# Attention followed by a GELU layer pair: batch 2 reordered in the GELU staging buffer, three transposes moved, left-over keys on VectorE, another start

## The chip, the cores and the metric

The kernel runs on 1 core of one Trainium2 chip. The metric is device microseconds of one execution. Times are medians of several runs. A ratio is the mean time of one kernel's fast runs over the mean of the other's fast runs in the same rounds, so it is not quite the ratio of the medians quoted beside it. "Chain of work" means the chain of instructions that ended last, followed back from the end.

## The reference, cut to what matters

```python
q, k, v: (8 batches, 12 heads, 448 positions, 64)      # float32
scores = q @ k^T / 8
attn = exp(scores - m) / (sum(exp(scores - m)) + exp(-m) + 1e-9)
x = (attn @ v) as 3584 rows of 768
h = x @ w_in                                            # 768 -> 2048
out = (0.5 * h * (1 + erf(h / sqrt 2))) @ w_out         # 2048 -> 768
```

## The kernel before: the parts that the change touches

Two heads make a pair, six pairs a batch, and a step is the attention of one pair, so there are 48 steps. 448 keys are three blocks of 128 and 64 left-over keys. Steps 1 to 6 (batch 0) are the opening. In later steps the two layers of the batch before lie between the parts of a step. Queries and keys of batches 0 and 1 are transposed by TensorE, those of later batches by DMA.

The start: the loads of the first two pairs, with the second pair held back behind small memsets, and narrow warm-up matmuls.

```python
    load_first(0, nc.sync, nc.scalar)          # pair 0: queries on the sync queue, keys on ScalarE's
    load_table(SET_LN_EXP)
    ...
    for t in (first_q[1], first_k[1]):
        nc.vector.memset(t[:, 0, 0, 0:1], 0.0)
    load_first(1, nc.sync, nc.sync)            # pair 1, after those memsets
    load_left(kl_raw, k, 0)                    # from here on GpSimd's queue
    ...
    for _ in range(54):
        nc.tensor.matmul(warm[0:D, 0:D], ones, ones, start=True, stop=True)
    ...
    load_q(1); load_k(1); load_left(kl_raw, k, 1)   # batch 1, ahead of all weights
    for i in range(4):
        load_w_in(i, 4)
```

One step of the opening. Denominators of the left-over keys come from a second pair of matmuls with `ones_left`:

```python
    def start_step(s):
        ps = presum_items(s)                   # six VectorE adds; the last two are the left-over keys
        for j in range(NK):
            scores(s, j)                       # and their exponentials on ScalarE
        if s >= 2:
            normalize(s - 2)
        ...
        if s + 1 < NPAIR:
            transpose_on_pe(0, s + 1)
        for c in {NPAIR - 2: (0,), NPAIR - 1: (1, 2, 3)}.get(s, ()):
            transpose_on_pe(1, c)
        ps[0](); ps[1]()
        scores_left(s)
        if s >= 1:
            values(s - 1)
            denominators(s - 1, left=et_t.pop(s - 1)[:, 2 * NK])
            log_den(s - 1)
            exp_den(s - 1)
        for p in ps[2:4]:
            p()
```

Batch 2 comes in by wide loads and is put in order by VectorE for the transposing DMA. Before, the ordered copy takes the raw buffer of batch 1, so batch 1 must be transposed completely by then:

```python
        if b not in ordered[w]:
            ordered[w][b] = raw_pool.tile([n, H, nj, D], FP16, name=name)
    ...
    step(NPAIR + 1, mlp1(0, 2, 6))
    transpose_on_pe(1, NPAIR - 1)
    gelu_window(0, 6)                          # first layer with its GELU, from a staging buffer "hbuf"
    fetch(0, -1)                               # orders the first half of batch 2
```

Only two PSUM buffers ("bank") serve transposes, values, denominators and both layers; three ("st") serve the scores.

The softmax here doesn't subtract the row's maximum and nothing guards it: scores larger than these inputs give would overflow.

## Time and profile before

| | kernel before |
|---|---|
| time | 416.02 us (415.27 to 416.29, 3 runs) |
| profiled run | 415.54 us, span 413.8 us |
| TensorE busy | 400.6 us (97%) |
| ScalarE busy | 300.5 us (73%) |
| VectorE busy | 196.0 us (47%) |
| GpSimd busy (issuing loads) | 102.2 us (25%) |

The page gives busy tenths for 40 slices of some 10 us; the slices in which TensorE's row is not full show where time can be won. A timeline line is: start, length, engine, source line, operation, output and inputs, shape, count, and in brackets how long the engine was idle just before and on whom it waited. The lines of the kernel before stand in the prediction below. Here is one more for later comparison, from the timeline of its TensorE: the key transposes of batch 1's first pair, with no wait on a load.

```profile
24.95 0.37 PE L243 MATMUL bank<-ident,rawk 128*64 128x128 f16 x6
```

### The profile page before, as it was taken

Reading aid. Unit: us, or ns where it says so; the run is one execution under the profiler, and the core shown is the slowest. Engines: PE = TensorE matmul, PEld = TensorE weight load, DVE = VectorE, ACT = ScalarE, POOL = GpSimd, SP = SyncE. Lnnn points to the kernel's source line nnn. Section 1 sums busy time; section 2 is a strip of 40 time slices with the busy share of each in tenths; the row PEclk is TensorE's granted clock in tenths of the full one; section 3 lists DMA queues with packets and bytes.
Section 4 is the critical chain, followed back from the end, with each engine's and each line's share of the span. In section 5 each row is a group of like instructions: output and inputs, shape, how many; then the busy total and the mean of one; then the engine's idle time right before and its main releaser. Section 6 shows DMA issues by size and latency. Waiting matters only on the chain.

```text
span 413.8 us, 10452 instructions
## 1 busy us (share of the span) xinstructions
PE 400.6 (97%) x4450; PEld 251.9 (61%) x4450; DVE 196.0 (47%) x471; ACT 300.5 (73%) x450; POOL 102.2 (25%) x137
## 2 busy tenths in 40 slices
PE   6789999999999999999999999999999999999996
PEld 4455755556556665556655566556566565687784
DVE  5666346873366604674256722576146741530021
ACT  5998779979897747978687766998588676734300
POOL 9732420674704540055201650020000000000000
PEclk9999999999999999999999999999999999999999
DMA  9999999999954996189921999159011100110022
GB/s 156 190 202 200 198 194 165 174 176 169 160 87 70 163 164 68 43 99 146 140 59 56 146 144 113 43 78 173 21 40 47 32 25 16 53 52 16 2 79 76
DMA packets 136671, 43.78 MB, mean 106 GB/s; under 512 B 117744, under 2 KB 136624, under 8 KB 136624
## 3 DMA queue, kind: packets, MB, share of 16 engines
q0 software_dynamic: 91440, 22.39, 58.1%
q1 hardware_dynamic: 44912, 20.52, 27.6%
q8 instruction: 35, 0.57, 0.6%
q10 hardware_dynamic: 272, 0.20, 0.1%
q14 instruction: 12, 0.10, 0.1%
HBM read 45.61 MB, written 11.01 MB: 137 GB/s over the span
## 4 chain that ended last, share of the span: by engine, by line
PE 90%; ACT 5%; DVE 2%; DMA 1%; issue 0%; SPq 0%; DVEq 0%
PE bank L230 73%; PE st L321 7%; PE bank L369 6%; ACT et L311 3%; PE st L230 2%; PE st L377 2%; DMA hbuf<-in_k_dram 1%; ACT rec L386 1%; ACT rec L389 1%; DVE xt L395 0%; DVE tqk L250 0%; ACT L72 0%; PE bank L238 0%; PE bank L243 0%; DVE vl L168 0%
## 5 line engine op out<-in xcount | busy, mean ns | idle before, releaser
L311 ACT ACTIVATE et<-st,expb 128x896 f16<-128x896 f32 x192 | 160.4, 913 | 34.1 <-PE st L321 25.6
L230 PE MATMUL bank<-xt,w_in_sb 128*64 128x448 f16 x1536 | 152.6, 353 | 0.5 <-DVE hbuf L423 0.3
L230 PEld LDWEIGHTS <-w_in_sb 128*64 128x64 f16 x1536 | 92.6, 110 | 56.2 <-issue 6.7
L230 PE MATMUL bank<-w_out_sb,gt_odd 128*64 128x384 f16 x1024 | 88.2, 327 | 0.0
L460 DVE COPY osb<-bank 128x384 f32<-128x384 f32 x56 | 31.2, 558 | 113.6 <-PE bank L230 113.6
L230 PEld LDWEIGHTS <-gt_odd 128*64 128x64 f16 x1024 | 60.6, 110 | 25.7 <-issue 4.5
L230 PE MATMUL bank<-w_out_sb,gt_even 128*64 128x384 f16 x768 | 68.9, 327 | 0.0
L395 DVE TENSOR_TENSOR xt<-bank,rec 128x448 f16<-128x448 f32 x48 | 29.8, 620 | 64.9 <-PE bank L369 46.6
L230 PEld LDWEIGHTS <-gt_even 128*64 128x64 f16 x768 | 43.5, 110 | 22.9 <-issue 4.4
L419 ACT ACTIVATE gt_odd<-bank 128x448 f16<-128x448 f32 (+1 forms) x74 | 29.1, 394 | 23.0 <-PE bank L230 21.9
L423 DVE COPY hbuf<-bank 128x448 f32<-128x448 f32 x54 | 33.7, 623 | 16.4 <-PE bank L230 15.2
L321 PE MATMUL st<-tqk 64*128 64x448 f16 x288 | 38.0, 362 | 1.8 <-ACT rec L386 0.7
L110 POOL DMA_DIRECT2D rawq<-in_q_dram x40 | 30.7, 786 | 35.5 <-DVE rawq L264 18.6
L369 PE MATMUL bank<-et,vn 128*64 128x448 f16 x288 | 35.5, 352 | 0.0
L355 DVE TENSOR_TENSOR t<-et 128x448 f16<-128x448 f16 x96 | 33.2, 388 | 2.5 <-ACT et L311 1.2
L355 DVE TENSOR_TENSOR ksum<-t,et 128x448 f16<-128x448 f16 x96 | 34.0, 384 | 0.6 <-ACT et L311 0.4
L419 ACT ACTIVATE gt_even<-bank 128x384 f16<-128x384 f32 x34 | 16.7, 490 | 23.0 <-PE bank L230 23.0
L355 DVE TENSOR_TENSOR ksum<-ksum,et 64x448 f16<-64x448 f16 x84 | 32.0, 382 | 1.3
L96 POOL DMA_DIRECT2D vn<-in_v_dram x9 | 8.9, 991 | 92.6 <-PE st L321 89.3
L110 POOL DMA_DIRECT2D rawk<-in_k_dram x30 | 24.6, 824 | 19.3 <-DMA rawq<-in_q_dram 15.3
L386 ACT ACTIVATE rec<-st,oneb 128x448 f32<-128x448 f32 x42 | 27.1, 647 | 2.8 <-PE st L377 2.8
L389 ACT ACTIVATE rec<-rec 128x448 f32<-128x448 f32 x48 | 27.6, 577 | 1.5
(58 smaller groups left out, 237.9 us busy)
## 6 DMA issues: line engine op xcount, KB each, us to landing
vn<-in_v_dram POOLq DMA_DIRECT2D x7, 576.0 KB, 9.1
rawq<-in_q_dram POOLq DMA_DIRECT2D x40, 84.0 KB, 10.7
rawk<-in_k_dram POOLq DMA_DIRECT2D x32, 96.0 KB, 8.0
w_in_sb<-in_moe_w_in_dram POOLq DMA_DIRECT2D x4, 768.0 KB, 18.8
w_out_sb<-in_moe_w_out_dram POOLq DMA_DIRECT2D x4, 768.0 KB, 21.3
out_dram<-osb SPq DMA_DIRECT2D x16, 168.0 KB, 3.7
out_dram<-osb SPq DMA_DIRECT2D x16, 144.0 KB, 2.1
out_dram<-osb SPq DMA_DIRECT2D x16, 120.0 KB, 2.0
```

The lines of the kernel that those rows point to most:

```text
L110: nc.gpsimd.dma_start(out=dst[:, :, j, e, :], in_=view[j, e])
L230: nc.tensor.matmul(out[x], lhs[:, x], rhs, start=start, stop=stop)
L311: nc.scalar.activation(out=out, in_=in_, func=AF.Exp, bias=expb, scale=scale)
L321: nc.tensor.matmul(st[:, e, 0:S], kt[r, j, :], qt[r], start=True, stop=True)
L355: nc.vector.tensor_tensor(out=dst, in0=a, in1=x, op=ALU.add)
L369: nc.tensor.matmul(po_t[g][e * D:(e + 1) * D, 0:S], v_t[b][:, 2 * c + e, j, :], et[:, 2 * j + e], start=False, stop=(j == NK - 1),)
L386: nc.scalar.activation(out=rec_t[g], in_=den_t.pop(g)[:, 0:S], func=AF.Ln, bias=oneb, scale=1.0)
L389: nc.scalar.activation(out=rec_t[g], in_=rec_t[g], func=AF.Exp, scale=-1.0)
L395: nc.vector.tensor_tensor(out=xt_t[b][:, c, :], in0=po_t.pop(g)[:, 0:S], in1=rec_t.pop(g), op=ALU.mult)
L419: nc.scalar.activation(out=dst[:, 0, :], in_=ph[:, c0:c1], func=AF.Gelu)
L423: nc.vector.tensor_copy(out=h_t[b][:, fc, :], in_=ph[:, 0:S])
L460: nc.vector.tensor_copy(out=osb, in_=po[:, 0:NHW])
```

## The change

Its intent: start the second pair's loads at once; keep the array's warm-up wide; take the left-over keys' denominators off TensorE; and put the ordered copy of batch 2 into the GELU staging buffer, so that batch 1's transposes can spread into later steps and the last of them lies beside the first second-layer item. The diff is cut to what matters. "Set n" below is the transposes of batch 1's pair n, counted from 0: `transpose_on_pe(1, n)`.

```diff
@@ load_pairs
         tiles[b] = raw_pool.tile([n, H, nj, D], FP16, name=name)
+        if b == 3:
+            nc.vector.memset(tiles[b][:, 0, 0, 0:1], 0.0)
@@ the start
-    load_first(0, nc.sync, nc.scalar)
-    load_table(SET_LN_EXP)
+    for i, queue in enumerate((nc.sync, nc.scalar)):
+        queue.dma_start(out=first_q[i], ...)
+        nc.scalar.dma_start(out=first_k[i], ...)
+        if i == 0:
+            load_table(SET_LN_EXP)
-    for t in (kl_raw[0], vl[0], kl_raw[1], vl[1]):
+    for t in (kl_raw[1], kl_raw[0], vl[0], vl[1]):          # now ahead of "ones"
         nc.vector.memset(t, 0.0)
-    ones_left = ...                                          # and its three memsets
-    for t in (first_q[1], first_k[1]):
-        nc.vector.memset(t[:, 0, 0, 0:1], 0.0)
-    load_first(1, nc.sync, nc.sync)
-    for _ in range(54):
-        nc.tensor.matmul(warm[0:D, 0:D], ones, ones, start=True, stop=True)
+    for _ in range(7):
+        nc.tensor.matmul(warm, kl_raw[1][:, 0],
+            kl_raw[1].rearrange("p c x -> p (c x)")[:, 0:512], start=True, stop=True)
@@ order_by_pairs
-        if b not in ordered[w]:
-            ordered[w][b] = raw_pool.tile([n, H, nj, D], FP16, name=name)
+        if b not in ordered[0]:
+            spare = h_pool.tile([P, 2 * NBURST * S], FP16, name="hbuf")
+            ...                                              # queries and keys side by side in it
@@ start_step
-        for c in {NPAIR - 2: (0,), NPAIR - 1: (1, 2, 3)}.get(s, ()):
+        for c in {NPAIR - 2: (0,), NPAIR - 1: (1, 2)}.get(s, ()):
-            denominators(s - 1, left=et_t.pop(s - 1)[:, 2 * NK])
+            denominators(s - 1)
-        for p in ps[2:4]:
+        for p in ps[2:]:
@@ the seventh and eighth step
-    transpose_on_pe(1, NPAIR - 2)
-    denominators(s - 1, left=et_t[s - 1][:, 2 * NK])
+    transpose_on_pe(1, NPAIR - 3)
+    denominators(s - 1)
+    transpose_on_pe(1, NPAIR - 2)
     step(NPAIR + 1, mlp1(0, 2, 6))
-    transpose_on_pe(1, NPAIR - 1)
@@ after the step with the first second-layer item
+        if b == 0 and r == 0:
+            transpose_on_pe(1, NPAIR - 1)
```

More of the change, by code (lines that the diff above doesn't have):

```diff
@@ L152 @@
         for n, nj, x, w in ((PS, NJ, 0, 512), (P, NK, 1024, 384)))
-    def load_first(i, queue_q, queue_k):
+    for i, queue in enumerate((nc.sync, nc.scalar)):
         h2 = slice(2 * i, 2 * i + 2)
-        queue_q.dma_start(
+        queue.dma_start(
             out=first_q[i], in_=q[0, h2, 0:PS * NJ].rearrange("h (p j) d -> p h j d", j=NJ))
-        queue_k.dma_start(
+        nc.scalar.dma_start(
             out=first_k[i], in_=k[0, h2, 0:P * NK].rearrange("h (p j) d -> p h j d", j=NK))
-    load_first(0, nc.sync, nc.scalar)
-    load_table(SET_LN_EXP)
+        if i == 0:
+            load_table(SET_LN_EXP)
     ident = const.tile([P, P], FP16, name="ident")
     make_identity(nc, ident)
+    for t in (kl_raw[1], kl_raw[0], vl[0], vl[1]):
+        nc.vector.memset(t, 0.0)
     ones = const.tile([P, D], FP16, name="ones")
     nc.vector.memset(ones, 1.0)
-    for t in (kl_raw[0], vl[0], kl_raw[1], vl[1]):
-        nc.vector.memset(t, 0.0)
-    ones_left = const.tile([P, P], FP16, name="ones_left")
-    nc.vector.memset(ones_left, 0.0)
-    for e in range(2):
-        r = slice(e * LEFT, (e + 1) * LEFT)
-        nc.vector.memset(ones_left[r, e * D:(e + 1) * D], 1.0)
     expb = const.tile([P, 1], FP32, name="expb")
@@ L186 @@
     warm = ps_bank.tile([P, 512], FP32, name="bank")
-    for _ in range(54):
-        nc.tensor.matmul(warm[0:D, 0:D], ones, ones, start=True, stop=True)
+    for _ in range(7):
+        nc.tensor.matmul(
+            warm, kl_raw[1][:, 0], kl_raw[1].rearrange("p c x -> p (c x)")[:, 0:512],
+            start=True, stop=True)
     load_v(0, 0, 4)
@@ L255, in order_by_pairs @@
     def order_by_pairs(b, w, c0, c1):
-        n, nj, raw, name = ((PS, NJ, q_raw, "rawq"), (P, NK, k_raw, "rawk"))[w]
-        if b not in ordered[w]:
-            ordered[w][b] = raw_pool.tile([n, H, nj, D], FP16, name=name)
+        nj, raw = ((NJ, q_raw), (NK, k_raw))[w]
+        if b not in ordered[0]:
+            spare = h_pool.tile([P, 2 * NBURST * S], FP16, name="hbuf")
+            for i, (rows, chunks, x) in enumerate(((PS, NJ, 0), (P, NK, H * NJ * D))):
+                ordered[i][b] = spare[0:rows, x:x + H * chunks * D].rearrange(
+                    "p (h j d) -> p h j d", h=H, j=chunks)
         src = raw[b].rearrange("p (c e) j d -> p c e j d", e=2)
@@ L363, in values @@
         b, c = divmod(g, NPAIR)
-        et = et_t.pop(g) if b else et_t[g]
+        et = et_t.pop(g)
         po_t[g] = ps_bank.tile([P, 512], FP32, name="bank")
@@ L372, in values, with denominators @@
                 )
-    def denominators(g, bank=None, left=None):
+    def denominators(g, bank=None):
         den_t[g] = ps_bank.tile([P, 512], FP32, name="bank") if bank is None else bank
@@ L378, in denominators @@
                 den_t[g][e * D:(e + 1) * D, 0:S], ones, sum_t[g][:, e, :],
-                start=True, stop=left is None)
-        if left is not None:
-            matmul_cols(den_t[g][:, 0:S], ones_left, left, False, True)
+                start=True, stop=True)
         del sum_t[g]
@@ L593 @@
     values(s - 1)
-    del et_t[s - 1]
     normalize(s - 1)
```

## The prediction

> **What bounds the kernel now.** I read the page first (busy tenths and clock), then the chain of work in order of time, then the timelines of the single engines in the stretches that the diff touches, and last the issue and landing times of the DMAs. The page's slices:
>
> ```profile
> span 413.8 us, 10452 instructions
> PE   6789999999999999999999999999999999999996
> ACT  5998779979897747978687766998588676734300
> PEclk9999999999999999999999999999999999999999
> ```
>
> TensorE is full from the fifth slice on (from about 40 us); only the first 40 us have holes. There the second row shows ScalarE near full. The chain for that part, pieces of it:
>
> ```profile
> 3.53 4.73 DMA hbuf<-in_k_dram
> 8.90 0.54 PE bank L243 x6
> 9.58 0.67 DVE tqk L250
> 10.30 1.30 PE st L321 x6
> ...
> 19.70 1.39 ACT et L311 x2
> ...
> 33.12 0.64 DVE xt L395
> 33.79 0.38 PE bank L377 x2
> 34.17 0.20 PE bank L230 x2
> 34.40 0.64 ACT rec L386
> ...
> 43.84 0.64 DVE hbuf L423
> 44.52 11.55 PE bank L230 x120
> ```
>
> (start, length, what). So there are four limits in turn: to 11 us the loads of the first heads, above all the second key load, which is only issued at 3.53 and lands at 8.27; to about 31 us ScalarE's exponentials; from 31 to 38 us a ping-pong in which ScalarE waits for TensorE; then TensorE to the end. A gain after 45 us needs less TensorE work or a closed hole; a gain before needs an earlier load or less ScalarE idle time. ScalarE at the start, with its idle time in brackets:
>
> ```profile
> 6.61 2.80 ACT L311 ACTIVATE et<-st,expb 128x896 f16<-128x896 f32 x3 [0.65 <-PE st L321]
> 9.96 0.63 ACT L311 ACTIVATE et<-st,expb 128x448 f16<-128x448 f32 x1 [0.54 <-PE st L230]
> 10.89 3.33 ACT L311 ACTIVATE et<-st,expb 128x896 f16<-128x896 f32 x4 [0.31 <-PE st L321]
> ```
>
> After the first exponential there are only 0.54 + 0.31 = 0.85 us of holes up to 31.6 us; the five later opening steps repeat every 4.345 us (19.61, 23.95, 28.30) without a hole. The two places further on where the diff can act:
>
> ```profile
> 33.79 0.38 PE L377 MATMUL bank<-ksum,ones 128*64 128x448 f16 x2 [0.65 <-DVE xt L395]
> 44.52 1.70 PE L230 MATMUL bank<-xt,w_in_sb 128*64 128x448 f16 x16 [0.29 <-DVE hbuf L423]
> 61.92 0.36 PE L321 MATMUL st<-tqk 64*128 64x448 f16 x2 [0.68 <-ACT rec L386]
> ```
>
> The last is a TensorE hole of 0.68 us right after the first second-layer item: the third score tile of the next step waits until the logarithm has given its bank back.
>
> **What the Trainium skill says.** "TensorE: Matmul & The Clock Gate", Part 1: the array starts at half rate and is released after a window of sustained activity of about 3.4 us. This trace agrees in kind, but its clock record shows 0.5 only up to 12.5 us although 54 narrow warm-up matmuls ran from 0.99 to 4.08; eight query transposes take 0.59 us before that and 0.40 after. "DMA: Bandwidth & Descriptors", section Issuing engines are not separate DMA queues: DMAs from all issuers interleave on the same 16 engines, so another issuing queue saves only issue time. Same page, section Queues, rings and completion order: each engine takes turns between queue rows. The trace fits: the first pair (224 and 192 KB, alone) landed in 3.3 and 3.6 us, the second, beside GpSimd's loads, in 4.3 and 4.7. "TensorEngine Tiling (Array Packing)", section Key Properties: tiles work independently. Here a pair of 64-column matmuls of 448 columns advances the chain by 0.19 us though each is recorded with some 0.35.
>
> **The change part by part.**
>
> *The start.* The second query load moves from the sync queue to ScalarE's queue and no longer waits for the small memsets at 3.05, and the second key load follows it. They sit behind the first key load on that queue, so the first pair should land as before (4.08 and 4.30), at worst some tenths later, because the second query load shares the engines with the tail of the first (224 against 192 KB: 32 KB). I take issue times of 1.3 to 2.9 us (the table load, 1.21 to 2.49, stands between in program order) instead of 3.16 and 3.53, and landings near 6 and 6.5 to 7 instead of 7.45 and 8.27. The transposes of pair 1 can then follow the scores of pair 0 directly at about 7.5 instead of 8.25 and 8.90. The left-over exponential of pair 0 would start when the three before it end (9.42, not 9.96) and those of pair 1 at 9.42 + 0.63 = 10.05, not 10.89. That is at most 0.85. The seven wide warm-up matmuls (512 columns at the slow rate, estimated from 448 columns in 0.38 to 0.43 us: about 3 us) start after the first 0.38 us memset, end near 4.3, before the first transposes at 4.78, and use the whole array, so the clock may be released well before 12.5; that would shorten the chain from landing to first exponential (transposes, scores: some 1.2 us of TensorE) by 0.2 to 0.4. Against it: the first left-over key load waits for the second memset now (about 0.4 later), and contention. Net: **-0.8 us**.
>
> *Left-over keys on VectorE.* Six steps lose two matmuls each, 0.19 us of TensorE per step, and gain two VectorE adds of 64x448, 0.38 each, 0.79 together. In steps 1 to 4 TensorE is not the limit, so nothing is gained. The adds fit: in the step at 18 us the partial sums end at 18.76, the left-over exponential at 18.57, the adds would run to 19.55, and the next VectorE work (normalize) starts at 19.73 behind the exponential of the logarithm. Slack 0.18 us, so no loss either. In the last two steps ScalarE does wait for the denominators (0.23 before 31.84 and 0.42 before 34.40), there 0.19 is won.
>
> *Transposes of batch 1.* Each set costs TensorE 0.56 us (29.11 to 29.67) and VectorE a copy of 0.65. Set 3 leaves the last opening step: the values at 30.48 and denominators at 31.23 come about 0.5 earlier and the 0.23 hole closes. With the 0.19 above, TensorE reaches the first layer about **0.4 us** earlier. Set 4 moves from the next step to just before the following one, set 5 from before the GELU stretch to after the first second-layer item. Between 34 and 56 us there is then one set as before (0.56), but ahead of work that waits for ScalarE anyway. Its copy waits behind four sums on VectorE (to about 39.9), so the second bank comes back late and layer-1 items two and three lose 0.1 to 0.3; in return the 0.29 hole at 44.24 and the bank wait at 43.4 vanish. **-0.2 us**. Set 5 falls just before the 0.68 us hole at 61.24: 0.56 less 0.68, nothing left over. Its copy should end near 62.2, when the next item (62.22) wants the bank: **0**.
>
> *Staging buffer.* The ordering copies wait for the GELU reads of the buffer (last one 51.6), but they wait for the query load anyway (53.14, after 7.80 us idle). The buffer is taken back by the first-layer copy at 86.71; the last transposing DMA landed at 84.88. Slack 1.8 us, more if that traffic thins: loads of batch 3 now start behind a VectorE memset, near 76.7 instead of 73.07, and finish perhaps 3 us later. They are needed at the scores at 118; their transposes landed at 107.5 and 109.7. **0**.
>
> Sum: -0.8 - 0.4 - 0.2 + 0 = -1.4; 416.0 - 1.4 = **414.6 us**.
>
> **The rivals.** (1) The second pair of loads delays the first. The old kernel plainly held it back on purpose. For it: all four are 832 KB, twice the data, and GpSimd's loads come on top. Against it: order on one queue. If both landings slip by 0.5 to 1 us, the first exponential slips by as much and the total is 415 to 416.2. (2) VectorE becomes the limit in the opening: 12 adds of 0.38 are 4.6 us more; if each step slipped by the 0.1 to 0.2 that the slack of 0.18 misses, five steps cost up to 1 us: about 415.5. VectorE is busy for 2.8 to 3.6 of each 5 us there, which speaks against it. (3) The staging buffer or the later batch-3 loads produce a new wait near 86 or 118 us. The slacks of 1.8 and about 8 us speak against it; a miss by 1 to 3 us would give 416 to 418. (4) Set 5 and its copy do not fit the hole: up to +0.6, so 415.2.
>
> **Range and chances.** The whole change acts in the first 90 us and on holes that sum to about 2.5 us; no part removes more. A gain of 2% (8.3 us) is not to be had, and a loss of 8 us would need a wait of which no trace line gives a hint. Range 413.3 to 416.3. Chances: faster 0.01, same 0.975, slower 0.015.
>
> **What would show it right or wrong.** The second key load lands before 7.3 and the hole before the 10.05 exponential is gone (start); the clock record rises before 12.5; ScalarE has no hole before the logarithm at about 31; the first-layer run that begins at 44.52 begins near 43; TensorE's hole near 61 holds the transposes of set 5 and the step after starts no later relative to the table load; no wait of the first-layer copy on a transposing DMA near 86; from 120 us on both traces are the same, shifted by about 1.4. Wrong: a first exponential later than 6.9, an opening period longer than 4.35, or a shift that appears only after 62 us.

## The result, and the profile after

The changed kernel took 414.47 us (413.94 to 415.48, 4 runs) against 415.84 us for the kernel before (4 runs, three of them those above): ratio 0.9971, interval 0.9947 to 0.9994. The predicted time was 414.6. Two later calls gave the changed kernel ratios of 0.9948 and 0.9959.

The profiled run was the slowest of the four (415.48 us). Its page:

```profile
span 413.7 us, 10346 instructions
PE   7778999999999999999999999999999999999996
ACT  6978879979897847978687766998588676734300
PEclk9989999999999999999999999999999999999999
```

From the fifth slice on the rows look as before (two digits of ScalarE's are one higher). The third slice has a dip in the clock row that was not there. ScalarE in the opening, from its timeline:

```profile
5.85 6.55 ACT L307 ACTIVATE et<-st,expb 128x896 f16<-128x896 f32 x8 [0.45 <-DVE rawq L295]
...
26.10 0.64 ACT L307 ACTIVATE et<-st,expb 128x448 f16<-128x448 f32 x1 [1.17 <-PE st L223]
27.96 0.63 ACT L380 ACTIVATE rec<-bank,oneb 128x448 f32<-128x448 f32 x1 [1.23 <-PE bank L373]
```

Eight exponentials run without a hole from 5.85, where before there were two holes and a start at 6.61: the start is won. But at 26 and 28 us there are two holes of 2.4 us in all that the kernel before did not have. TensorE shows what they wait for:

```profile
24.68 0.54 PE L236 MATMUL bank<-ident,rawk 128*64 128x128 f16 x6 [1.33 <-DMA rawk<-in_k_dram]
```

These are the same transposes as the line at 24.95 above. Now they wait 1.33 us for batch 1's keys, which landed at 24.64 us (22.77 before), and by the clock record the array runs at half clock from 24.47 to 27.88, one window of 3.4 us. From these transposes to the next step's scores TensorE took 27.86 - 24.68 = 3.18 us, before it was 26.64 - 24.95 = 1.69: the half clock costs about as much again as the wait. TensorE's transposes and the scores behind them, and so ScalarE, are late. So in this one pair of traces the start's gain was lost again by 29 us: the sixth step's exponentials begin at 29.11 against 28.30.

Further on, from the timelines of TensorE and of GpSimd's queue:

```profile
59.62 0.39 PE L231 MATMUL bank<-ident,rawq 112*64 112x112 f16 x8
...
61.87 0.37 PE L317 MATMUL st<-tqk 64*128 64x448 f16 x2 [0.38 <-ACT rec L380]
```

```profile
77.18 6.08 POOL L112 DMA_DIRECT2D rawq<-in_q_dram  x8 [20.81 <-DVE xt L389]
```

Set 5 stands at 59.62, and the hole behind it has shrunk from 0.68 to 0.38 us. Batch 3's loads start at 77.18 instead of 73.07, behind the new memset, and nothing waits for it. And on VectorE in the opening:

```profile
16.87 0.80 DVE L351 TENSOR_TENSOR ksum<-ksum,et 64x448 f16<-64x448 f16 x2
17.92 0.62 DVE L389 TENSOR_TENSOR xt<-bank,rec 128x448 f16<-128x448 f32 x1 [0.25 <-ACT rec L383]
```

The two adds of the left-over keys end at 17.67, 0.25 before the normalization that they might have delayed.

### The profile page after: what moved, and what is told of

Its sections match the earlier page's. It is cut to its first block, busy times and chain, and to the rows that moved or that the text cites. A ratio compares the mean times of both kernels' runs of the same rounds, so it can differ in the third digit from the quotient of the medians.

```text
span 413.7 us, 10346 instructions
## 1 busy us (share of the span) xinstructions
PE 399.0 (96%) x4391; PEld 249.4 (60%) x4391; DVE 199.8 (48%) x480; ACT 300.7 (73%) x450; POOL 102.1 (25%) x137
## 4 chain that ended last, share of the span: by engine, by line
PE 90%; DMA 3%; ACT 3%; POOL 3%; DVE 1%; issue 0%
PE bank L223 73%; PE st L317 6%; PE bank L365 6%; DMA klraw<-in_k_dram 3%; PE st L223 2%; PE st L373 2%; ACT et L307 2%; POOL rawk L96 1%; POOL rawq L96 1%; POOL klraw L117 0%; ACT rec L380 0%; POOL vl L117 0%; ACT L72 0%; ACT rec L383 0%; POOL vn L96 0%
## 5 line engine op out<-in xcount | busy, mean ns | idle before, releaser
L351 DVE TENSOR_TENSOR ksum<-ksum,et 64x448 f16<-64x448 f16 x96 | 36.6, 381 | 1.5
```

Of the source, the lines that this page charges most:

```text
L351: nc.vector.tensor_tensor(out=dst, in0=a, in1=x, op=ALU.add)
```

## The experiments

The first pair of traces left a question. The measured time fits the forecast, but in those traces the start was lost again by 29 us. Theory A: the start gains more than 1 us, and the order of the loads (batch 1's keys) takes a part of it back. Theory B: that trace was a slow one by chance. Theory C: the gain comes from the rest of the change, and the start gives nothing.

Eleven runs were made; each was correct. Each "edit" is against the kernel that is named. One thing helps in reading them: the time after the opening hardly varies. From the second exponential of the seventh step to the end it is 378.25 us in the first trace of the kernel before (413.8 less 35.55).

**The changed kernel again.** No edit.

> The changed kernel a second time, to see how much of its first trace was chance. That trace had exponentials of the third step at 13.44 us instead of 15.26 (gain 1.8 us), but then TensorE waited 1.33 us for batch 1's keys, which landed at 24.64 instead of 22.77, and ran at half clock for 3.4 us. Theory A (the opening became bound by the order of the loads): the wait is there again, keys of batch 1 land at 24 to 25 us, and ScalarE stands still for over 1.5 us between 24 and 29. Theory B (that trace was a slow one by chance): keys land below 23.2 us, the wait is under 0.8 us, and the span is near 412.5. Time in both: 414.3 us, ratio to before 0.996 to 0.998.

Measured: 414.45 us, ratio 0.9948 (0.9936 to 0.9959). TensorE at the same place:

```profile
24.73 0.36 PE L236 MATMUL bank<-ident,rawk 128*64 128x128 f16 x6 [0.31 <-DMA rawk<-in_k_dram]
```

The keys landed at 24.69, as in theory A, but the wait is 0.31: in this run the first pair's keys came in at 4.92 (4.00 in the first trace), so the whole opening ran 1.1 us later (third step's exponentials at 14.53, not 13.44) and met the keys when they were nearly there. ScalarE's lost time is 0.28 us, not over 1.5. Both theories hold a part: the late keys are the rule, the full 2.4 us were a bad case.

**The wide warm-up alone.**

```diff
(kernel before)
-    for _ in range(54):
-        nc.tensor.matmul(warm[0:D, 0:D], ones, ones, start=True, stop=True)
+    for _ in range(7):
+        nc.tensor.matmul(warm, kl_raw[1][:, 0], <512 columns of kl_raw[1]>, start=True, stop=True)
```

> The kernel before with the wide warm-up matmuls alone (and the memset order they need). If the clock is what brings the start forward: clock record full from about 4 us instead of 12.5, first exponential near 6.0 instead of 6.61, exponentials of pair 1 near 10.2 instead of 10.89, since the second loads still land at 7.5 and 8.3. Time 0.4 to 0.7 us below before (ratio 0.9985) if nothing takes it back; ratio 1.000 if the batch-1 keys bind.

Measured: 416.48 us, ratio 0.9999 (0.9985 to 1.0012). A miss in the trace: the clock was full from 5.19 for one window only, then half until 15.43, and the second pair's keys landed at 9.20. ScalarE:

```profile
10.77 0.63 ACT L313 ACTIVATE et<-st,expb 128x448 f16<-128x448 f32 x1 [1.65 <-PE st L232]
...
15.81 0.63 ACT L388 ACTIVATE rec<-bank,oneb 128x448 f32<-128x448 f32 x1 [0.78 <-PE bank L232]
```

The edit also reorders the memsets, and GpSimd's first left-over key load, which waits for one of them, was issued at 1.99 instead of 1.66 us; the second half of these keys landed at 8.31 instead of 6.42, and TensorE waited 1.53 us for them (whether for this reason is not shown). So the wide warm-up with the order of memsets that it needs gives nothing that can be measured; the width by itself was not run.

**The early second pair alone.**

```diff
(kernel before)
     load_first(0, nc.sync, nc.scalar)
     load_table(SET_LN_EXP)
+    load_first(1, nc.scalar, nc.scalar)
-    for t in (first_q[1], first_k[1]):
-        nc.vector.memset(t[:, 0, 0, 0:1], 0.0)
-    load_first(1, nc.sync, nc.sync)
```

> The kernel before with the second pair of loads alone on ScalarE's queue and not held back. If the early loads are what brings the start forward: they land near 5 and 6 us, first exponential still near 6.6 (clock low until 12 us), the 0.54 and 0.31 us holes gone, pair 1's exponentials at 10.05. Rival: first pair lands later by 0.5 us or more. Time 0.5 to 0.85 us below before (ratio 0.998) if nothing takes it back; 1.000 if the batch-1 keys bind.

Measured: 415.12 us, ratio 0.9972 (0.9952 to 0.9992), 1.2 us. The first pair's keys landed at 4.96 (4.30 to 4.34 in the two traces of the kernel before), so the feared contention is real, about 0.6 us; the second pair landed at 5.75 and 6.86. ScalarE:

```profile
6.53 6.72 ACT L309 ACTIVATE et<-st,expb 128x896 f16<-128x896 f32 x8 [0.60 <-PE st L319]
14.20 0.63 ACT L384 ACTIVATE rec<-bank,oneb 128x448 f32<-128x448 f32 x1 [0.95 <-PE bank L228]
```

The holes of 0.54 and 0.31 are gone. In this trace a new hole of 0.95 before the first logarithm took the gain back: with the clock low until 14.0, TensorE had not finished the denominators with their second pair. Theory C falls: the early loads alone bring the time down.

**The rest without the start.**

```diff
(changed kernel)
-    the new start: all four first loads at once, wide warm-up, memset order
+    the old start: pair 1 held back, narrow warm-up, old memset order
```

> The changed kernel with the old start (narrow warm-up, second pair held back): left-over keys on VectorE, transposes moved, staging buffer alone. My working says 0.6 us below before: 0.4 in the ping-pong at 31 to 38 us (holes of 0.23 and 0.42 before the logarithms shrink), 0.2 at the entry of the GELU stretch. Ratio 0.9985. Rival (the adds on VectorE slow GpSimd's loads): batch 1's keys land after 23.8 us instead of 22.77 here too, and the packets between 10 and 15 us fall from 2270 to below 1900; if the slow loads came from the start or chance they land at 22.5 to 23.2.

Measured: 415.23 us, ratio 0.9969 (0.9957 to 0.9981), 1.3 us, more than the 0.6 expected. The changed kernel took 414.45, so inside the whole change the start is worth 0.8 us. Keys of batch 1 landed at 23.66, between the two forecasts (after 23.8, or 22.5 to 23.2), with 1926 packets between 10 and 15 us, above the rival's 1900: this run doesn't decide it. The next runs do.

**The kernel before, a second trace.** No edit; one look.

> The kernel before itself, for a second trace of it. Its first trace had batch 1's keys landed at 22.77 us; the four traces of the changed and part kernels had 23.66 to 24.90. If that first trace was a lucky one, the keys land above 23.5 us here, and the packets between 10 and 15 us are below 2000 instead of 2270; if the old order of work really gives faster loads, about 22.8 again. The clock record should show a short release (one window of 3.4 us) at a chance place or none before 12 us.

Measured: 415.59 us. The trace repeats the first within 0.05 us at ScalarE's marks (sixth step's exponentials at 28.34). Keys of batch 1 landed at 23.05, with 2144 packets between 10 and 15 us, nearer to the forecast of faster loads than to that of luck. Both traces of the kernel before move more packets there than every other trace (1547 to 2088), and have the keys earlier than every other one in which they were not cut in halves (23.66 to 24.90 us). The adds on VectorE are not needed for the slower loads, for the runs with the warm-up or the early loads alone have no adds in the opening and landed at 24.90 and 24.54. Why the loads between 10 and 15 us are slower there stays open. Also, both traces of the kernel before are of quick executions (415.54 and 415.59); in the three calls its medians were 416.68, 416.13 and 416.29. So its traces understate what the change gains, and the times decide, not the pair of traces. They are also of one kind only: their mean clock is 0.998 and 1.000, while 18 of this kernel's 33 executions have 0.990 or 0.991, the value (0.988 to 0.992) of every trace here whose clock came up early and fell back for 6.8 us. None of the changed kernel's 15 executions has it (0.994 to 1.000). No trace shows the kernel before in that kind; the two kinds differ in mean time by 0.6 us in one call and by nothing in another, so what share of the gain is the clock's stays open.

**The left-over keys alone.**

```diff
(kernel before)
-            denominators(s - 1, left=et_t.pop(s - 1)[:, 2 * NK])
+            denominators(s - 1)
-        for p in ps[2:4]:
+        for p in ps[2:]:
-    ones_left ... and its memsets
```

> The kernel before with only the left-over keys summed on VectorE in the opening. My working: 0.19 us in each of the last two opening steps where ScalarE waits for the denominators, the hole of 0.42 before the logarithm shrinks to about 0.23, the hole of 0.23 to 0.04; plus up to 0.4 in the second step when the clock is still low there. Time 0.3 to 0.6 us below before, ratio 0.999.

Measured: 415.32 us, ratio 0.9981 (0.9965 to 0.9998), 0.8 us.

```profile
32.26 0.64 ACT L381 ACTIVATE rec<-bank,oneb 128x448 f32<-128x448 f32 x1
...
34.63 0.64 ACT L381 ACTIVATE rec<-bank,oneb 128x448 f32<-128x448 f32 x1 [0.23 <-PE bank L372]
```

The hole of 0.23 that stood before 31.84 is gone, the one of 0.42 is 0.23: exactly the working. From the sixth step's exponentials (28.91) to the second one of the seventh (35.79) it took 6.88 us instead of 7.25, so 0.37.

**The moves alone.** Staging buffer, memset for batch 3 and the three transposes.

```diff
(kernel before)
+    the hunks load_pairs, order_by_pairs and all transpose_on_pe(1, ...) of the change, nothing else
```

> The kernel before with only the staging buffer and the moved transposes. In the two traces with all of the rest, the stretch from the exponentials of the sixth step to the first of the seventh took 6.72 instead of 7.25 us, and the remainder 377.84 instead of 378.25. If the moves carry most of it: hole of 0.23 gone, ratio 0.998 to 0.9985 (0.6 to 0.8 us); if the left-over keys carry it, ratio near 1.000.

Measured: 415.69 us, ratio 0.9985 (0.9968 to 1.0003), 0.6 us.

```profile
32.46 0.65 ACT L391 ACTIVATE rec<-bank,oneb 128x448 f32<-128x448 f32 x1
...
35.03 0.63 ACT L391 ACTIVATE rec<-bank,oneb 128x448 f32<-128x448 f32 x1 [0.42 <-PE bank L232]
```

Here the first hole (0.23) is gone and the second (0.42) stays: the mirror of the run before. From 29.27 to 36.18 it took 6.91 us, so 0.34 less than 7.25. The interval of the time just includes no change, but the stretches are sharp: with both parts they are 6.72 or 6.73 in all three traces of the changed kernel.

**Batch 1 in two halves.**

```diff
(changed kernel)
-    load_q(1)
-    load_k(1)
-    load_left(kl_raw, k, 1)
+    load_q(1, 0, H // 2)
+    load_k(1, 0, H // 2)
+    load_left(kl_raw, k, 1)
+    load_q(1, H // 2, H)
+    load_k(1, H // 2, H)
```

> The changed kernel with batch 1's queries and keys loaded in two halves, the half and the left-over keys that the fifth step transposes first. If the order of the loads is what now binds at 24 us: first half's keys land near 20 to 21 us, TensorE has no DMA wait at 23 to 25 us, ScalarE no hole between 22 and 31 us, and the time falls by 0.4 to 1.3 us below the changed kernel's 414.45 (ratio to before 0.992 to 0.994). If it does not bind: ratio 0.9948 as the changed kernel.

Measured: 414.24 us, ratio 0.9954 (0.9939 to 0.9969). The first half of the keys landed at 20.86, the wait and the holes are gone, and the sixth step's exponentials begin at 26.94: the early part is as expected and shows that the order of loads was the cause of that wait. The time isn't: no better than the changed kernel. From the seventh step to the end it took 378.7 us instead of 377.9. VectorE and TensorE near 72 us:

```profile
71.48 0.81 DVE L262 COPY hbuf<-rawk 128x576 f16<-128x576 f16 x2 [0.78 <-DMA rawk<-in_k_dram]
```

```profile
72.88 0.38 PE L225 MATMUL bank<-et,vl 128*64 128x448 f16 x2 [0.50 <-DVE xt L391]
```

The ordering copy of batch 2's last keys waits for their load (landed at 71.46), the normalization stands behind it on VectorE, and TensorE waits for the bank that this gives back. The gain became a wait on the next load.

**That load earlier.**

```diff
(kernel of the run before)
-    for i in range(2):
-        load_w_out(1, i, 2)
     load_q(2, half, H)
     load_k(2, half, H)
+    for i in range(2):
+        load_w_out(1, i, 2)
```

> The changed kernel with batch 1's queries and keys in two halves, as in the run before, and also the second halves of batch 2's queries and keys loaded ahead of the last two weight loads. In the run before, the opening was won (first exponentials of the seventh step at 33.67 instead of 34.68 to 35.84 us) but 0.9 us of it was lost again later: TensorE waited 0.50 us at 72.88 and 0.20 at 58.26 behind VectorE's ordering copies, which waited for batch 2's last keys (landed at 71.46). If that wait is what took the gain back: the last keys of batch 2 land near 63 us, no hole at 72.88, the rest from the seventh step's exponentials takes 377.8 to 378.0 us instead of 378.7, and the time is 0.5 to 1 us below the halves alone (ratio to before 0.992 to 0.994). If not: 0.995 to 0.996 as the halves alone.

Measured: 414.97 us, ratio 0.9967 (0.9951 to 0.9983), a miss. The last keys landed at 59.64 and the hole at 72.88 is gone, but 379.5 us passed from the seventh step to the end:

```profile
73.79 0.74 PE L319 MATMUL st<-tqk 64*128 64x448 f16 x6 [0.31 <-ACT rec L385]
...
76.77 0.38 PE L225 MATMUL st<-tqk 128*64 128x448 f16 x2 [0.81 <-DMA tqk<-klraw]
```

Now the transposing DMA of batch 2's left-over keys comes late. These two waits are 1.1 of the 1.7 us by which 379.5 exceeds the changed kernel's 377.9; the rest was not traced to a cause. Neither kernel that starts sooner beats the changed one.

**The changed kernel with the narrow warm-up.**

```diff
(changed kernel)
-    for _ in range(7): <wide matmuls on kl_raw[1]>
+    for _ in range(54):
+        nc.tensor.matmul(warm[0:D, 0:D], ones, ones, start=True, stop=True)
     and the old order of "ones" and the four memsets
```

> The changed kernel with the old narrow warm-up (and the memset order that goes with it). If the wide matmuls matter beside the early loads: clock dropped again after one window, third step's exponentials about 1 us later than with them, ratio to before worse by 0.001 to 0.002 than the changed kernel of the same call. If the release of the clock is chance and the wide warm-up does nothing (as the run with it alone showed: 0.9999): the same ratio.

Measured: 414.31 us, ratio 0.9952 (0.9937 to 0.9967): the same as with the wide one. The clock came up at 8.81 and stayed. The keys of batch 1 landed at 23.66, just ahead of their use, with no wait:

```profile
23.93 0.37 PE L234 MATMUL bank<-ident,rawk 128*64 128x128 f16 x6
```

This trace reached the seventh step's second exponential at 33.99, 1.85 us before the first trace of the changed kernel, and its span is only 1.5 us shorter: here too part is lost again, between 55 and 82 us. In this trace, too, the ordering copy of batch 2's last keys waits for its load (0.26 us, landed at 71.10).

**The changed kernel a third time.** No edit.

> The changed kernel again, as the measure for the two others on this chip. Ratio to before 0.9945 to 0.9975. A third trace of it: batch 1's keys land at 24 to 25 us, TensorE waits for them for 0.3 to 1.3 us if its clock was released early.

Measured: 414.33 us, ratio 0.9959 (0.9940 to 0.9978). Its clock was up from 5.04 (and at half for one window from 25.52), keys of batch 1 landed at 24.33, and:

```profile
24.38 0.36 PE L236 MATMUL bank<-ident,rawk 128*64 128x128 f16 x6 [0.74 <-DMA rawk<-in_k_dram]
```

Three traces of one kernel, three waits: 1.33, 0.31, 0.74 us. The sooner the opening runs, the longer the wait. That is theory A in kind; its figure for ScalarE's idle time (over 1.5 us) held in the first trace alone.

The marks of all traces, in us from the start of the span:

| trace | pair 1's keys land | third step's exponentials | batch 1's first keys land | sixth step's exponentials | from there to the second one of the seventh step |
|---|---|---|---|---|---|
| before | 8.27 | 15.26 | 22.77 | 28.30 | 7.25 |
| before again | 8.30 | 15.28 | 23.05 | 28.34 | 7.25 |
| changed | 5.90 | 13.44 | 24.64 | 29.11 | 6.73 |
| changed again | 6.53 | 14.53 | 24.69 | 27.96 | 6.72 |
| changed, third | 6.37 | 13.73 | 24.33 | 28.43 | 6.72 |
| wide warm-up alone | 9.20 | 16.96 | 24.90 | 30.00 | 7.25 |
| early pair alone | 6.86 | 15.34 | 24.54 | 28.39 | 7.24 |
| rest without start | 8.21 | 15.80 | 23.66 | 28.84 | 6.72 |
| left-over keys alone | 8.14 | 15.73 | 24.30 | 28.91 | 6.88 |
| moves alone | 8.50 | 16.23 | 23.94 | 29.27 | 6.91 |
| batch 1 in halves | 6.60 | 13.90 | 20.86 | 26.94 | 6.73 |
| and batch 2 earlier | 6.50 | 13.96 | 21.17 | 27.17 | 6.71 |
| changed, narrow warm-up | 6.31 | 14.23 | 23.66 | 27.28 | 6.71 |

## Why the prediction was right, step by step

The forecast of 414.6 us and "within 2%" held, with 414.47, 414.45 and 414.33 us measured. The gain was 1.4 us on the first chip run and 2.0 to 2.2 us later, by the medians (1.2, and 1.7 to 2.2, by the ratios). That the forecast hits to 0.2 us is in part luck: it starts from 416.02 for the kernel before, whose medians later were 416.1 to 416.7, and the gain there is larger than the 1.4 forecast. The start was given 0.8 and measures 0.8 inside the change; the rest was given 0.6 and measures 1.3 (0.8 to 1.8), so the second is the term that was mis-sized. Of the terms:

- *The start, -0.8: about right as a net, wrong in its make-up.* The landings were estimated at 6 and 6.5 to 7 and came at 4.8 to 5.9 and 5.9 to 6.5; the table load did not hold up the queue (the second query load was issued at 1.25). The two holes went as worked out. The third step's exponentials came 0.7 to 1.8 us sooner than in the traces before, in two of three traces by more than the 0.85 allowed for. What failed is a step that was not there: the working asked whether the second pair delays the first, and not whether the loads behind them keep up. Batch 1's keys were the next limit. Their wait, with the half-clock window beside it in two of the three traces, took back between 0.3 (ScalarE idle in the second trace) and 2.4 us. Run alone, the early loads are worth 1.2 us.
- *The warm-up, 0.2 to 0.4 within the start: wrong.* Alone 0.9999; exchanged in the changed kernel 0.9952 against 0.9959. The prediction also overstated its source. The record of the clock begins, in the trace of before, with full speed at 12.5 us; that it was half until then I read from the durations (0.59 against 0.40 us). The wide matmuls did not by themselves keep the clock up: the trace with them alone fell back. What went with a clock that stays up is how busy TensorE was in the window of 3.4 us after the release: 0.42 to 0.49 of it in the four traces with an early release and the second pair held back, 0.51 in the one with the early pair alone, and all five fell back; 0.70 to 0.81 in the four of the changed kernel and its halves, and none did. So the early loads may also gain through the clock; no run separates this share.
- *Left-over keys, 0.19 in each of two steps: right.* 0.37 measured. That nothing is gained in steps 1 to 4 was worked out for a clock that is up. With the clock low there was a hole before the first logarithm, of 0.56, 0.78 and 0.95 us in the three such traces with the second pair of matmuls and of 0.60 and 0.61 in the two without it: no gain is shown there either.
- *Set 3 out of the last opening step: right, a little small.* The hole of 0.23 closed in the run with the moves alone, 0.34 us there. Together with the left-over keys it is 7.25 - 6.72 = 0.53, where 0.4 was given; it is not 0.37 + 0.34, because both shorten the same hole of 0.23.
- *Sets 4 and 5, -0.2 and 0: mis-sized and right.* From the seventh step's second exponential to the first second-layer item it took 56.67 - 35.55 = 21.12 us before and 56.61 - 35.84 = 20.77 after: -0.35. As forecast, the bank wait and the hole before 44.52 are gone: the first layer's matmuls run unbroken from 40.83 to 56.0 us. From there to the next item it took 62.22 - 56.67 = 5.55 and 62.16 - 56.61 = 5.55: set 5 used the hole and cost nothing.
- *Staging buffer, 0: right.* In the changed trace the transposing DMA of batch 2's last keys landed at 85.56 and the first-layer copy that takes the buffer back ran at 86.66 without a wait; the slack was 1.1 us, not 1.8 or more. From 62.2 us to the end both traces take the same time (413.8 - 62.22 = 351.6 and 413.7 - 62.16 = 351.5).
- *The signs.* "No hole before the logarithm at about 31" came true. "The same from 120 us on, shifted by about 1.4" came true for the times and not for the one pair of traces (shift 0.1), because that pair joins a quick execution of the kernel before to the slowest of the four of the changed one. Two signs of being wrong came true as well. The opening period from the fifth to the sixth step was 6.97, 4.74 and 6.00 us in the three traces of the changed kernel, not 4.35, by the wait for batch 1's keys; and in the second trace the first exponential began at 6.94, later than 6.9, since the first keys landed at 4.92. So the prediction was right in its number and in most terms, and its own sign told of the limit that it had missed.

Of the rivals, the first (contention) is real: in six of the seven traces with early loads the first keys landed at 4.59 to 4.96 us against 4.30 to 4.34 in the two of the kernel before, so 0.3 to 0.65 us later (in the first trace of the changed kernel at 4.00); it is outweighed. The second (VectorE the limit in the opening) did not happen: the slack of the adds was 0.25 us. The third and fourth did not happen in the changed kernel.

What remains open: why the loads between 10 and 15 us move fewer packets in all other traces than in the two of the kernel before (these two are also the only ones with the second pair held back in which the clock did not come up early and fall back, so kernel and clock are not separated); and what share of the 1.2 us of the early loads a kernel with other loads behind them would keep.

## What to carry to other kernels

When a change pulls the start forward, follow the queue of loads behind it to the point where each is first used: the next load that is just in time takes the gain back, and after that the next one, as batch 1's and then batch 2's keys did here. A wait of TensorE can cost more than its length: after the one of 1.33 us the array ran at half clock for 3.4 us. A stretch that hardly varies from run to run (here 6.72 against 7.25 us) can settle terms of a few tenths that the total time, with runs 2 us apart, cannot. One pair of traces is one draw: check which end of the spread each of them comes from before reading the difference.

## What the Trainium skill lacked or had wrong

- "TensorE: Matmul & The Clock Gate", Part 1, says that the release depends on where the free-running window of 3413 ns falls and varies from run to run. The runs agree: the short stretches of the clock were 3.413, 6.827, 13.653 or 20.480 us long, and in the three traces of the changed kernel the first full record begins at 3.99, 5.04 and 10.47 us. What it lacks is how much work holds the clock up: after some 3 us of unbroken warm-up it was released at 3.8 to 5.9 us in nine of thirteen traces, but in five of those it fell back after one window to half speed for 6.8 us, both with 54 narrow and with 7 wide matmuls; in the other four the first full record begins only at 8.8 to 12.5 us. Cutting the thirteen traces into windows of 3.413 us in step with their clock records gives a figure: in the windows before the nine falls to half speed (leaving out the end of the program) TensorE was busy for only 0.41 to 0.60 of the time, for instance 1.39 of 3.42 us from 21.05 to 24.47 in the first trace of the changed kernel; of the 1489 full-speed windows after which the clock stayed up, two were at 0.60 and all others at 0.63 or more. (Busy is the union of the matmuls' records, whose ends are modelled.)
- "DMA: Bandwidth & Descriptors", section Issuing engines are not separate DMA queues, says that another issuing queue saves only the time of issue. Here the issue came 1.9 us sooner (1.25 instead of 3.16 us) because the load no longer waited for memsets, worth 1.2 us together with the other queue; no run separates the two. That section doesn't say whether a table load on ScalarE holds up a DMA that follows it in the program; here it didn't (table load 1.22 to 2.50, issue at 1.25).
- The same page, section Queues, rings and completion order, tells how engines take turns between queue rows, but gives no figure for the cost to a load that is under way. Here the first keys landed 0.3 to 0.6 us later (4.59 to 4.96 against 4.30 to 4.34) in six of the seven traces in which a second pair followed at once, and 0.3 us sooner (4.00) in the seventh.
